# Moving the modulation and query weight loads of a decode attention kernel

## The chip, the cores and the metric

The kernel runs on one core of a Trainium2 chip. The metric is the device time of one execution in microseconds (us); a smaller number is better. The span of an execution is the time from its first to its last instruction in the profile. Heads are counted from 0, so the last one is head 31. Times are medians of several executions. A ratio of two kernels is the mean time of one kernel's runs over that of the other's runs of the same rounds on the same chip, so it is not quite the ratio of the medians that stand beside it.

Engine names in the profile lines: PE is the matrix engine (PEld its weight loads), DVE the vector engine, ACT the scalar engine, POOL the fourth compute engine, SPq the queue of the engine that issues all DMAs here.

## The reference

One token (batch 1, one position, D = 640) goes through one transformer block. Modulation vectors come from a conditioning vector `c`. Attention has 32 heads with their own K and V of 16384 positions and 128 channels, so K and V are 268 MB of the 290 MB that are read.

```python
mod = (silu(c) @ w_mod).reshape(1, 6, 1, 640)          # w_mod: 640 x 3840
sa, ca, ga, sb, cb, gb = (mod[:, i] for i in range(6))
h = layernorm(A_x) * (1 + ca) + sa
q = h @ wq                                             # wq: 640 x 4096, 32 heads of 128
p = softmax(q . k_cache * 128**-0.5)                   # per head, 16384 positions
x = A_x + ga * ((p @ v_cache) @ wo)                    # wo: 4096 x 640
h = layernorm(x) * (1 + cb) + sb
x = x + gb * ((silu(h @ w_gate) * (h @ w_up)) @ w_down)   # 640 x 1728 twice, 1728 x 640
```

Only `sa` and `ca` (the first third of `w_mod`) are needed before attention. `ga`, `sb`, `cb`, `gb` are needed after the last head.

## The kernel before

The program is a list of operations with a position and their dependencies; each engine executes its own in order of position. All DMAs go through one queue, in order, and wait there for the buffers they overwrite. Head `h` has base position `T0 + h * PERIOD`. K and V have two buffers each. DVE multiplies K by the query (in place), folds 128 channels down and reduces; ACT makes the exponent; PE multiplies by V.

```python
# weight region, shared over time
wmod_v = wreg[:, 0:WM_E]...                 # all of w_mod: 2/6 early, 4/6 later
wq_v = [wreg[:, WM_E + i*WQ_E : ...] for i in range(2)]   # ring of two, 4 heads each
wg_v, wu_v, wd_v = ...                      # gate, up, down overlay the same region at the end

d_c  = plan.dma(0.0, c_col[:], c_in[0].rearrange("(c p) -> p c", p=128), "c", noncontig=True)
d_x  = plan.dma(0.1, x_col[:], A_x[0, 0].rearrange("(c p) -> p c", p=128), "x", noncontig=True)
d_wm = plan.dma(0.2, wmod_v[:, :, 0:NA*128], wm_src[:, :, 0:NA*128], "wm")
d_wq[0] = plan.dma(0.3, wq_v[0], wq_src(0), ("wq", 0))
# ...
TB = T0 + 2 * PERIOD - 4.0
d_wm_b = plan.dma(TB, wmod_v[:, :, NA*128:], wm_src[:, :, NA*128:], "wmb")        # about head 4
o_mod_b = op(PE, TBC, lambda e: f_mod(e, NA, NMOD), deps=[d_wm_b, o_sc, o_modc_a])
# ...
for b in range(NQB):                        # 8 blocks of 4 heads: rows of 512 elements, 1024 bytes
    if b > 0:
        d_wq[b] = plan.dma(max(q_pos(b) - 30.0, 1.0), wq_v[b % 2], wq_src(b), ("wq", b % 2), deps=deps)
    o_qmm[b] = op(PE, q_pos(b), f_q, deps=[d_wq[b], o_h])
# ...
for h in range(H):
    d_k[h] = [plan.dma(... base - 25.0, kring[:, s2], kv(A_k, h), ("k", s2), deps=[o_fold1[h - 2]])]
    d_v[h] = [plan.dma(base - 4.9 ..., vring[:, s2, ...], ..., deps=[o_pvlast[h - 2]])]
    d_wo[h] = plan.dma(base + 1.5, woring[:, s2], A_wo[h*128:(h+1)*128, :], ...)
# ... after the last head:
o_abf = op(ACT, TE, ... attn_bf <- attn_ps)            # attention output, then ga, x1, layernorm 2
o_gu = op(PE, TE + 1.2, f_gu, deps=[o_h2, d_wg, d_wu, o_zg, o_zu])
o_dn = op(PE, TE + 1.8, f_down, deps=[o_gum, d_wd, d_wd2])
```

## Time and profile before

| | before |
|---|---|
| time, median of the first 5 runs (range) | 702.09 us (701.16 to 702.38) |
| span in the profiled run | 700.7 us |
| DMA queue's share of 16 engines | 98.1% |
| DVE busy | 618.5 us (88%) |
| first multiply of the last head begins | 652.15 us |
| from there to the end | 48.5 us |

These lines are from the profile page of the kernel before. The digits are the busy share, in tenths, of 40 equal slices of the span; GB/s is what the 16 DMA engines moved in each slice.

```profile
span 700.7 us, 4866 instructions
DMA  7999999999999999999999999999999999999992
GB/s 283 447 428 412 418 430 433 434 420 427 427 437 426 423 428 427 428 424 430 428 427 427 432 427 430 422 434 422 428 430 430 418 430 432 430 430 430 407 402 97
DMA packets 26096, 290.79 MB, mean 415 GB/s; under 512 B 3226, under 2 KB 14170, under 8 KB 16730
q1 hardware_dynamic: 26074, 290.48, 98.1%
...
wreg<-in_A_wq_dram SPq DMA_DIRECT2D x8, 640.0 KB, 29.7
...
wreg<-in_w_mod_dram SPq DMA_DIRECT2D x1, 3200.0 KB, 25.8
```

The reader should see a DMA queue that is full from the second slice to the last but one. While that holds, the time at which a given load lands is set by how much DMA work stands before it in the queue. In the last two lines the columns are the number of loads, KB each, and us from issue to landing.

The trace also records each DMA packet. Grouped by size (mean duration; the sum divided by the 16 engines; left out are the 3456-byte rows of gate and up, 11.2 us, and the 8 KB rows of the K and V loads that come in pieces, 30.2 us):

| packet | what | count before | mean ns | us of 16 engines |
|---|---|---|---|---|
| 2 B | c, x | 1280 | 8 | 0.7 |
| 1024 B | wq | 5120 | 50 | 16.0 |
| 1280 B | wo, w_down | 5824 | 57 | 20.6 |
| 2560 B | w_mod, early part | 640 | 108 | 4.3 |
| 5120 B | w_mod, late part | 640 | 201 | 8.0 |
| 32 KB | K, V | 7808 | 1220 | 595.5 |

The end of the run decides the rest. These are lines of the timeline of the kernel before (start us, duration us, engine, line, operation, output<-input, shapes, count, and in brackets how long the engine had been idle and what ended that):

```profile
652.15 8.69 DVE L410 TENSOR_TENSOR kring<-kring,qbc_sb 128x16384 bf16<-128x16384 bf16 x1 [0.52 <-DMA kring<-in_A_k_cache_dram]
...
673.16 6.72 PE L449 MATMUL psb<-vring,P_sb 128*4 128x512 bf16 x16
680.03 3.92 PE L449 MATMUL psb<-vring,P_sb 128*4 128x512 bf16 x16
...
686.03 0.29 PE L472 MATMUL psb<-On,woring 128*128 128x1 bf16 x5 [0.36 <-ACT On L465]
686.37 0.18 ACT L490 ACTIVATE attn_bf<-psb 128x5 bf16<-128x5 f32 x1 [0.39 <-PE psb L472]
689.56 4.43 PE L513 MATMUL psb<-h_col,wreg 128*128 128x1 bf16 x140 [3.23 <-DVE h_col L500]
695.16 2.83 PE L528 MATMUL psb<-gu_col,wreg 128*128 128x1 bf16 x70 [1.17 <-DVE gu_col L521]
```

The last head's multiply starts 0.5 us after DVE went idle, because its K has just landed. From there a compute chain runs to the end, and gate/up (L513) and down (L528) wait for activations, not for weights. So the time is "when the last K lands" plus a tail of 48.5 us in which the DMA queue still has V and the FFN weights to bring.

### The profile page before, as it was taken

The numbers are of one execution on the slowest core, as the hardware profiler recorded it, in microseconds if no ns is written. First come the engines' busy times: TensorE is split into PE (matmuls) and PEld (weight loads), VectorE is DVE, ScalarE is ACT, GpSimd is POOL, SyncE is SP. The second block draws the span as 40 slices with busy tenths as digits, with TensorE's granted clock in tenths as the row PEclk, the third lists the DMA queues.
The fourth block names the chain that finished last, engine by engine and source line by source line (L and its number), as shares of the span: only waits on it lengthen the run. The fifth ranks groups of instructions, "written<-read, shape, count | busy, mean of one in ns | idle before, by whom it ended". The sixth has DMA issues, their size and how long they took to land.

```text
span 700.7 us, 4866 instructions
## 1 busy us (share of the span) xinstructions
PE 365.1 (52%) x1993; PEld 154.3 (22%) x1993; DVE 618.5 (88%) x220; ACT 84.5 (12%) x321; POOL 251.1 (36%) x76
## 2 busy tenths in 40 slices
PE   0006666644566644446665525665444566555755
PEld 0002223212222211222221212222212222222314
DVE  0799989998999899998999988998999989999931
ACT  1100110111011101111110110111011111101101
POOL 0056633340433354443334404333044433344400
PEclk9999677876776667666666767766676666667975
DMA  7999999999999999999999999999999999999992
GB/s 283 447 428 412 418 430 433 434 420 427 427 437 426 423 428 427 428 424 430 428 427 427 432 427 430 422 434 422 428 430 430 418 430 432 430 430 430 407 402 97
DMA packets 26096, 290.79 MB, mean 415 GB/s; under 512 B 3226, under 2 KB 14170, under 8 KB 16730
## 3 DMA queue, kind: packets, MB, share of 16 engines
q1 hardware_dynamic: 26074, 290.48, 98.1%
q8 instruction: 15, 0.25, 0.1%
q14 instruction: 7, 0.06, 0.0%
HBM read 290.47 MB, written 0.00 MB: 415 GB/s over the span
## 4 chain that ended last, share of the span: by engine, by line
DMA 48%; DVE 39%; PE 6%; issue 3%; POOL 3%; ACT 1%; POOLq 0%; DVEq 0%
DMA kring<-in_A_k_cache_dram 48%; DVE kring L410 22%; DVE f L412 11%; PE psb L449 4%; DVE f L422 3%; POOL Ls L437 2%; DVE S_sb L424 2%; PE psb L513 1%; PE psb L528 0%; ACT acc_sb L455 0%; ACT P_sb L434 0%; POOL gm L430 0%; PE psb L461 0%; ACT R_sb L393 0%; DVE pm L427 0%
## 5 line engine op out<-in xcount | busy, mean ns | idle before, releaser
L449 PE MATMUL psb<-vring,P_sb 128*4 128x512 bf16 x1024 | 298.4, 462 | 29.1 <-DMA vring<-in_A_v_cache_dram 28.2
L410 DVE TENSOR_TENSOR kring<-kring,qbc_sb 128x16384 bf16<-128x16384 bf16 (+1 forms) x35 | 278.6, 7960 | 31.2 <-DMA kring<-in_A_k_cache_dram 27.7
L437 POOL PARTITION_ALL_REDUCE Ls<-rs x32 | 212.3, 6634 | 41.9 <-ACT P_sb L434 41.9
L430 POOL PARTITION_ALL_REDUCE gm<-pm x32 | 36.3, 1136 | 364.1 <-DVE pm L427 353.6
L449 PEld LDWEIGHTS psb<-vring,P_sb 128*4 128x4 bf16 x1024 | 97.6, 98 | 217.3 <-issue 104.6
L412 DVE TENSOR_TENSOR f<-kring 128x8192 bf16<-128x8192 bf16 (+1 forms) x35 | 142.1, 4059 | 1.2
L396 PE MATMUL psb<-R_sb,ones_bf 128*128 128x128 bf16 x32 | 9.2, 286 | 233.9 <-ACT R_sb L393 233.9
L422 DVE TENSOR_TENSOR f<-f 128x4096 bf16<-128x4096 bf16 x64 | 112.5, 1758 | 2.2
L424 DVE TENSOR_REDUCE S_sb<-f 128x128 f32<-128x2048 bf16 x32 | 73.1, 2286 | 1.1
L396 PEld LDWEIGHTS psb<-R_sb,ones_bf 128*128 128x128 bf16 x32 | 3.3, 104 | 236.8 <-ACT R_sb L393 236.8
L455 ACT ACTIVATE acc_sb<-psb 4x512 f32<-4x512 f32 x32 | 18.7, 583 | 244.4 <-PE psb L449 244.4
L461 PE MATMUL psb<-identf,acc_sb 4*128 4x1 f32 x256 | 33.9, 249 | 23.7 <-ACT acc_sb L455 23.7
L461 PEld LDWEIGHTS psb<-identf,acc_sb 4*128 4x128 f32 x256 | 31.2, 188 | 37.0 <-ACT acc_sb L455 37.0
L439 ACT ACTIVATE lnl<-Ls 128x1 f32<-128x1 f32 x32 | 6.5, 202 | 198.2 <-POOL Ls L437 198.2
L472 PE MATMUL psb<-On,woring 128*128 128x1 bf16 x160 | 9.1, 167 | 23.6 <-ACT On L465 23.6
L491 DVE TENSOR_TENSOR tt<-attn_bf,mod_col 128x5 f32<-128x5 bf16 x1 | 0.2, 166 | 15.0 <-ACT attn_bf L490 15.0
L434 ACT ACTIVATE P_sb<-S_sb,nb 128x128 bf16<-128x128 f32 x32 | 12.8, 401 | 1.0
L393 ACT ACTIVATE R_sb<-ident,q_r 128x128 bf16<-128x128 bf16 x32 | 12.4, 386 | 0.0
L472 PEld LDWEIGHTS psb<-On,woring 128*128 128x128 bf16 x160 | 6.4, 101 | 26.3 <-ACT On L465 26.3
L302 DVE TENSOR_SCALAR xc<-x_f,st 128x5 f32<-128x5 f32 x1 | 0.2, 231 | 13.0 <-POOL st L299 13.0
L432 ACT ACTIVATE nb<-gm 128x1 f32<-128x1 f32 x32 | 6.2, 195 | 44.3 <-POOL gm L430 44.3
L399 ACT ACTIVATE qbc_sb<-psb 128x128 bf16<-128x128 f32 x32 | 8.9, 278 | 12.1 <-PE psb L396 12.1
(59 smaller groups left out, 76.5 us busy)
## 6 DMA issues: line engine op xcount, KB each, us to landing
kring<-in_A_k_cache_dram SPq DMA_DIRECT2D x31, 4096.0 KB, 26.7
vring<-in_A_v_cache_dram SPq DMA_DIRECT2D x30, 4096.0 KB, 30.7
vring<-in_A_v_cache_dram SPq DMA_DIRECT2D x8, 1024.0 KB, 21.5
wreg<-in_A_wq_dram SPq DMA_DIRECT2D x8, 640.0 KB, 29.7
woring<-in_A_wo_dram SPq DMA_DIRECT2D x32, 160.0 KB, 28.6
kring<-in_A_k_cache_dram SPq DMA_DIRECT2D x4, 1024.0 KB, 13.4
wreg<-in_w_mod_dram SPq DMA_DIRECT2D x1, 3200.0 KB, 25.8
wreg<-in_B_w_gate_dram SPq DMA_DIRECT2D x1, 2160.0 KB, 24.7
```

What stands on the lines that cost most here:

```text
L396: o_qbcmm[h] = op(PE, base - 14.8 if h > 0 else 2.7, lambda e, s2=s2: e.matmul(qbc_ps[s2], lhsT=ones_bf[:], rhs=R_sb[:, s2], start=True, s ...
L410: o_m = op(DVE, base + 3.3 * c, lambda e, ksl=ksl, qb=qb: e.tensor_tensor(out=ksl, in0=ksl, in1=qb, op=ALU.mult), deps=[d_k[h][c], o_qbc[h ...
L412: o_f = op(DVE, base + 3.3 * c + 2.2 + (6.6 if npc == 1 else 0.0), lambda e, ksl=ksl, c=c, KP=KP: e.tensor_tensor(out=f1[:, c * KP:(c + 1) ...
L422: prev = op(DVE, base + 13.3 + i, lambda e, w=w: e.tensor_tensor(out=f1[:, :, 0:w], in0=f1[:, :, 0:w], in1=f1[:, :, w:2 * w], op=ALU.add), ...
L424: o_red[h] = op(DVE, base + 17.0, lambda e, w=w, s2=s2: e.tensor_reduce(out=S_sb[:, s2], in_=f1[:, :, 0:w], axis=AX.X, op=ALU.add), deps=[ ...
L430: o_gm[h] = op(POOL, base + 19.6, lambda e, h=h: e.partition_all_reduce(gm[:, h:h + 1], pm[:, h:h + 1], channels=128, reduce_op=bass.bass_ ...
L434: o_exp[h] = op(ACT, base + 20.4, lambda e, h=h, s2=s2: e.activation(out=P_sb[:, s2], in_=S_sb[:, s2], func=ACTF.Exp, scale=SCALE, bias=nb ...
L437: o_L[h] = op(POOL, base + 21.0, lambda e, h=h: e.partition_all_reduce(Ls[:, h:h + 1], rs[:, h:h + 1], channels=128, reduce_op=bass.bass_i ...
L449: last = e.matmul(acc_ps[s2], lhsT=P_sb[:, s2, 4 * j:4 * j + 4], rhs=vring[:, s2, 4 * j:4 * j + 4, :].rearrange("p a d -> p (a d)"), start ...
L455: o_acc[h] = op(ACT, base + 39.5, lambda e, s2=s2: e.activation(out=acc_sb[:, s2, :], in_=acc_ps[s2], func=ACTF.Copy), deps=[o_pvlast[h], ...
L461: last = e.matmul(OT_ps[:, h:h + 1], lhsT=acc_sb[:, s2, 128 * i:128 * (i + 1)], rhs=identf[:, i:i + 1], start=(i == 0), stop=(i == 3))
L472: last = e.matmul(attn_ps[:, cc:cc + 1], lhsT=woring[:, s2, 128 * cc:128 * (cc + 1)], rhs=On[:, h:h + 1], start=(h == 0 and cc == 0), stop ...
```

## The change

The intent: make `wq` two loads instead of eight (4 heads, then the other 28 with 7168-byte rows); start with `w_mod` instead of the tiny `c` and `x`; load the late four sixths of `w_mod` after the last K into the K buffer that is then free; split the down projection so that it can start on most of its weights. The core of the diff, with cuts:

```diff
-        wmod_v = wreg[:, 0:WM_E]...
-        wq_v = [wreg[:, WM_E + i * WQ_E: ...]... for i in range(2)]
+        wma_v = wreg[:, 0:WMA_E]...
+        wq0_v = wreg[:, WMA_E:WMA_E + WQ0_E]...
+        wqr_v = wreg[:, 0:WQR_E]... if H > HB else None
+            wmb_v = kring[:, (H - 2) % 2]...[:, 0:WMB_E]...
...
-        d_c = plan.dma(0.0, c_col[:], ...)
-        d_x = plan.dma(0.1, x_col[:], ...)
-        d_wm = plan.dma(0.2, wmod_v[:, :, 0:NA * 128], ...)
-        d_wq[0] = plan.dma(0.3, wq_v[0], wq_src(0), ("wq", 0), ...)
+        d_wm = plan.dma(0.0, wma_v, wm_src[:, :, 0:2 * D], "wm", ...)
+        d_c = plan.dma(0.1, c_col[:], ...)
+        d_x = plan.dma(0.15, x_col[:], ...)
+        d_wq0 = plan.dma(0.3, wq0_v, wq_src[:, :, 0:HB * 128], "wq0", ...)
...
-        TB = T0 + 2 * PERIOD - 4.0
+            TB = TLAST + 2.0              # TLAST: base of the last head
+            TBC = TLAST + 41.5
...
+            d_wqr = plan.dma(2.3, wqr_v, wq_src[:, :, HB * 128:H * 128], "wqr", deps=[o_mod, o_qmm0], ...)
+            o_qmm1, o_qbf1, o_qr1 = q_ops(TQR, wqr_v, HB, H, d_wqr, "1")
...
+        d_wm_b = plan.dma(TB, wmb_v, wm_src[:, :, 2 * D:6 * D], "wmb", deps=[o_fold1[H - 2]], ...)
+        o_mod_b = op(PE, TBC, lambda e: f_mod(e, wmb_v, NA, NMOD, NA), deps=[d_wm_b] + mb_deps, ...)
...
-        o_dn = op(PE, TE + 1.8, f_down, deps=[o_gum, d_wd, d_wd2], name="down")
+        o_dn_a = op(PE, TE + 1.8, lambda e: f_down(e, 0, nA), deps=[o_gum, d_wd], name="down_a")
+        o_dn = op(PE, TE + 1.85, lambda e: f_down(e, nA, FCH), deps=[o_dn_a, d_wd_b, d_wd2], name="down")
```

More of the change, by code (lines that the diff above doesn't have):

```diff
@@ L180, in build @@
         x_col = sb("x_col", [128, KC], BF16)
-        WM_E = KC * 6 * D
-        WQ_E = KC * HB * 128
-        WREG_E = max(WM_E + 2 * WQ_E, 2 * KC * F + FCH * D)
+        LATE_MB = (TT * 128 >= KC * 4 * D) and H >= 3
+        NA = 2 * KC
+        WMA_E = KC * 2 * D
+        WQ0_E = KC * HB * 128
+        WQR_E = KC * (H - HB) * 128
+        WMB_E = KC * 4 * D
+        FFN_E = 2 * KC * F + FCH * D
+        WREG_E = max(WMA_E + WQ0_E, WQR_E, FFN_E) + (0 if LATE_MB else WMB_E)
         wreg = sb("wreg", [128, WREG_E], BF16)
-        wmod_v = wreg[:, 0:WM_E].rearrange("p (k n) -> p k n", k=KC)
-        wq_v = [wreg[:, WM_E + i * WQ_E: WM_E + (i + 1) * WQ_E].rearrange("p (k n) -> p k n", k=KC) for i in range(2)]
+        wma_v = wreg[:, 0:WMA_E].rearrange("p (k n) -> p k n", k=KC)
+        wq0_v = wreg[:, WMA_E:WMA_E + WQ0_E].rearrange("p (k n) -> p k n", k=KC)
+        wqr_v = wreg[:, 0:WQR_E].rearrange("p (k n) -> p k n", k=KC) if H > HB else None
         wg_v = wreg[:, 0:KC * F].rearrange("p (k n) -> p k n", k=KC)
@@ L190, in build @@
         kring = sb("kring", [128, 2, TT, 128], BF16)
+        if LATE_MB:
+            wmb_v = kring[:, (H - 2) % 2].rearrange("p t d -> p (t d)")[:, 0:WMB_E].rearrange("p (k n) -> p k n", k=KC)
+        else:
+            wmb_v = wreg[:, WREG_E - WMB_E:WREG_E].rearrange("p (k n) -> p k n", k=KC)
         vring = sb("vring", [128, 2, TT, 128], BF16)
@@ L260, in build @@
             fill=0.0, base=0, channel_multiplier=-1), deps=[o_onesf], name="identf")
-        d_c = plan.dma(0.0, c_col[:], c_in[0].rearrange("(c p) -> p c", p=128), "c", noncontig=True, name="dma_c")
-        d_x = plan.dma(0.1, x_col[:], A_x[0, 0].rearrange("(c p) -> p c", p=128), "x", noncontig=True, name="dma_x")
-        NA = 2 * KC
         wm_src = w_mod.rearrange("(k p) n -> p k n", p=128)
-        d_wm = plan.dma(0.2, wmod_v[:, :, 0:NA * 128], wm_src[:, :, 0:NA * 128], "wm", name="dma_wmod_a")
-        def wq_src(b):
-            return A_wq[:, b * HB * 128:(b + 1) * HB * 128].rearrange("(k p) n -> p k n", p=128)
-        d_wq = [None] * NQB
-        d_wq[0] = plan.dma(0.3, wq_v[0], wq_src(0), ("wq", 0), name="dma_wq0")
+        d_wm = plan.dma(0.0, wma_v, wm_src[:, :, 0:2 * D], "wm", name="dma_wmod_a")
+        d_c = plan.dma(0.1, c_col[:], c_in[0].rearrange("(c p) -> p c", p=128), "c", noncontig=True, name="dma_c")
+        d_x = plan.dma(0.15, x_col[:], A_x[0, 0].rearrange("(c p) -> p c", p=128), "x", noncontig=True, name="dma_x")
+        wq_src = A_wq.rearrange("(k p) n -> p k n", p=128)
+        d_wq0 = plan.dma(0.3, wq0_v, wq_src[:, :, 0:HB * 128], "wq0", name="dma_wq0")
         o_tbl = op(ACT, 0.0, lambda e: e.preload_act_table_set("natural_log_exp_and_others"), name="tbl")
@@ L278, in build, with f_mod @@
         o_sc = op(DVE, 0.5, lambda e: e.tensor_tensor(out=silu_c[:], in0=c_col[:], in1=rr[:], op=ALU.mult), deps=[o_rr], name="silu_c")
-        def f_mod(e, j0, j1):
+        def f_mod(e, wv, j0, j1, jofs):
             last = None
@@ L283, in f_mod @@
                 for k in range(KC):
-                    last = e.matmul(mod_ps[:, j:j + 1], lhsT=wmod_v[:, k, 128 * j:128 * (j + 1)], rhs=silu_c[:, k:k + 1],
+                    last = e.matmul(mod_ps[:, j:j + 1], lhsT=wv[:, k, 128 * (j - jofs):128 * (j - jofs + 1)], rhs=silu_c[:, k:k + 1],
                                     start=(k == 0), stop=(k == KC - 1))
             return last
-        o_mod = op(PE, 1.0, lambda e: f_mod(e, 0, NA), deps=[d_wm, o_sc], name="mod_mm_a")
+        o_mod = op(PE, 1.0, lambda e: f_mod(e, wma_v, 0, NA, 0), deps=[d_wm, o_sc], name="mod_mm_a")
         o_modc_a = op(ACT, 1.5, lambda e: e.activation(out=mod_col[:, 0:NA], in_=mod_ps[:, 0:NA], func=ACTF.Copy), deps=[o_mod], name="mod_col_a")
-        TB = T0 + 2 * PERIOD - 4.0
-        d_wm_b = plan.dma(TB, wmod_v[:, :, NA * 128:], wm_src[:, :, NA * 128:], "wmb", name="dma_wmod_b")
-        TBC = min(TB + 2.5 * PERIOD, T0 + H * PERIOD - 8.0)
-        o_mod_b = op(PE, TBC, lambda e: f_mod(e, NA, NMOD), deps=[d_wm_b, o_sc, o_modc_a], name="mod_mm_b")
-        o_modc = op(ACT, TBC + 0.2, lambda e: e.activation(out=mod_col[:, NA:], in_=mod_ps[:, NA:NMOD], func=ACTF.Copy), deps=[o_mod_b], name="mod_col_b")
+        TLAST = T0 + (H - 1) * PERIOD
+        if LATE_MB:
+            TB = TLAST + 2.0
+            TBC = TLAST + 41.5
+        else:
+            TB = T0 + 2 * PERIOD - 4.0
+            TBC = min(TB + 2.5 * PERIOD, T0 + H * PERIOD - 8.0)
+        mb_deps = [o_sc, o_modc_a]
+        d_wm_b = None
         o_onep = op(DVE, 1.6, lambda e: e.tensor_scalar_add(out=onep[:, 0, :], in0=mod_col[:, KC:2 * KC], scalar1=1.0), deps=[o_modc_a], name="onep_a")
-        o_onep_b = op(DVE, TBC + 5.0, lambda e: e.tensor_scalar_add(out=onep[:, 1, :], in0=mod_col[:, 4 * KC:5 * KC], scalar1=1.0), deps=[o_modc], name="onep_b")
+        o_onep_b_pos = TBC + 0.4
         def layernorm_ops(pos, src_f32, src_dep, rs_col, tag, xc_t, want_rs=None):
@@ L323, in build @@
         o_h = op(DVE, 1.8, lambda e: e.tensor_tensor(out=h_col[:], in0=tt1[:], in1=mod_col[:, 0:KC], op=ALU.add), deps=[o_t1, o_modc_a], name="h_col")
-        o_qmm = [None] * NQB
-        o_qbf = [None] * NQB
-        o_qr = [None] * NQB
-        def q_pos(b):
-            return 2.0 if b == 0 else T0 + b * HB * PERIOD - 22.0
-        for b in range(NQB):
-            if b > 0:
-                deps = [o_qmm[b - 2]] if b >= 2 else []
-                d_wq[b] = plan.dma(max(q_pos(b) - 30.0, 1.0), wq_v[b % 2], wq_src(b), ("wq", b % 2), deps=deps, name="dma_wq%d" % b)
-            def f_q(e, b=b):
-                last = None
-                for hl in range(HB):
-                    hh = b * HB + hl
-                    for k in range(KC):
-                        last = e.matmul(q_ps[:, hh:hh + 1], lhsT=wq_v[b % 2][:, k, 128 * hl:128 * (hl + 1)], rhs=h_col[:, k:k + 1],
-                                        start=(k == 0), stop=(k == KC - 1))
-                return last
-            o_qmm[b] = op(PE, q_pos(b), f_q, deps=[d_wq[b], o_h], name="q_mm%d" % b)
-            o_qbf[b] = op(ACT, q_pos(b) + 0.1, lambda e, b=b: e.activation(
-                out=q_bf[:, b * HB:(b + 1) * HB], in_=q_ps[:, b * HB:(b + 1) * HB], func=ACTF.Copy), deps=[o_qmm[b]], name="q_bf%d" % b)
-            o_qr[b] = op(ACT, q_pos(b) + 0.2, lambda e, b=b: e.activation(
-                out=q_r32[:, b * HB:(b + 1) * HB], in_=q_bf[:, b * HB:(b + 1) * HB], func=ACTF.Copy), deps=[o_qbf[b]], name="q_r32_%d" % b)
@@ new lines, in f_q, with q_ops @@
+        def f_q(e, wv, h0, h1):
+            last = None
+            for hh in range(h0, h1):
+                for k in range(KC):
+                    last = e.matmul(q_ps[:, hh:hh + 1], lhsT=wv[:, k, 128 * (hh - h0):128 * (hh - h0 + 1)], rhs=h_col[:, k:k + 1],
+                                    start=(k == 0), stop=(k == KC - 1))
+            return last
+        def q_ops(pos, wv, h0, h1, ddep, tag):
+            o_mm = op(PE, pos, lambda e: f_q(e, wv, h0, h1), deps=[ddep, o_h], name="q_mm" + tag)
+            o_bf = op(ACT, pos + 0.1, lambda e: e.activation(out=q_bf[:, h0:h1], in_=q_ps[:, h0:h1], func=ACTF.Copy), deps=[o_mm], name="q_bf" + tag)
+            o_r = op(ACT, pos + 0.2, lambda e: e.activation(out=q_r32[:, h0:h1], in_=q_bf[:, h0:h1], func=ACTF.Copy), deps=[o_bf], name="q_r32_" + tag)
+            return o_mm, o_bf, o_r
@@ new lines, in build @@
+        o_qmm0, o_qbf0, o_qr0 = q_ops(2.0, wq0_v, 0, HB, d_wq0, "0")
+        o_qmm_last, o_qbf_last = o_qmm0, o_qbf0
+        o_qr = [o_qr0] * H
+        if H > HB:
+            TQR = T0 + 0.6 * PERIOD
+            d_wqr = plan.dma(2.3, wqr_v, wq_src[:, :, HB * 128:H * 128], "wqr", deps=[o_mod, o_qmm0], name="dma_wq_rest")
+            o_qmm1, o_qbf1, o_qr1 = q_ops(TQR, wqr_v, HB, H, d_wqr, "1")
+            for hh in range(HB, H):
+                o_qr[hh] = o_qr1
+            o_qmm_last, o_qbf_last = o_qmm1, o_qbf1
+            assert T0 + HB * PERIOD - 15.0 > TQR + 0.3
@@ L394, in build @@
                 out=R_sb[:, s2], in_=ident[:], func=ACTF.Copy, scale=q_r32[:, h:h + 1]),
-                deps=[o_qr[b], o_ident, o_qbcmm[h - 2] if h >= 2 else None], name="R%d" % h)
+                deps=[o_qr[h], o_ident, o_qbcmm[h - 2] if h >= 2 else None], name="R%d" % h)
             o_qbcmm[h] = op(PE, base - 14.8 if h > 0 else 2.7, lambda e, s2=s2: e.matmul(
@@ L477, in build @@
         TE = T0 + (H - 1) * PERIOD + 42.0
-        TW = max(T0 + (H - 1) * PERIOD + 2.0, q_pos(NQB - 1) + 0.5, TBC + 0.5)
-        wdeps = [o_qmm[NQB - 1], o_mod_b]
+        d_wm_b = plan.dma(TB, wmb_v, wm_src[:, :, 2 * D:6 * D], "wmb",
+                          deps=[o_fold1[H - 2]] if LATE_MB else [], name="dma_wmod_b")
+        o_mod_b = op(PE, TBC, lambda e: f_mod(e, wmb_v, NA, NMOD, NA), deps=[d_wm_b] + mb_deps, name="mod_mm_b")
+        o_modc = op(ACT, TBC + 0.2, lambda e: e.activation(out=mod_col[:, NA:], in_=mod_ps[:, NA:NMOD], func=ACTF.Copy), deps=[o_mod_b], name="mod_col_b")
+        o_onep_b = op(DVE, o_onep_b_pos, lambda e: e.tensor_scalar_add(out=onep[:, 1, :], in0=mod_col[:, 4 * KC:5 * KC], scalar1=1.0), deps=[o_modc], name="onep_b")
+        TW = TLAST + 2.5 if LATE_MB else max(TLAST + 2.5, TBC + 0.5)
+        wdeps = [o_qmm_last, o_mod] + ([] if LATE_MB else [o_mod_b])
         d_wg = plan.dma(TW, wg_v, B_wg.rearrange("(k p) n -> p k n", p=128), "wg", deps=wdeps, name="dma_wg")
@@ L482, in build @@
         nfull = FCH - 1 if FLAST < 128 else FCH
-        d_wd = plan.dma(TW + 0.02, wd_v[:, 0:nfull, :], B_wd[0:nfull * 128, :].rearrange("(k p) n -> p k n", p=128), "wd",
-                        deps=wdeps, name="dma_wd")
+        nA = max(1, nfull - 1)
+        wd_src = lambda k0, k1: B_wd[k0 * 128:k1 * 128, :].rearrange("(k p) n -> p k n", p=128)
+        d_wd = plan.dma(TW + 0.02, wd_v[:, 0:nA, :], wd_src(0, nA), "wd", deps=wdeps, name="dma_wd")
+        d_wd_b = plan.dma(TW + 0.03, wd_v[:, nA:nfull, :], wd_src(nA, nfull), "wdb", deps=wdeps, name="dma_wd_b") if nfull > nA else None
         d_wd2 = None
         if nfull < FCH:
-            d_wd2 = plan.dma(TW + 0.03, wd_v[0:FLAST, nfull, :], B_wd[nfull * 128:F, :], "wd2",
+            d_wd2 = plan.dma(TW + 0.04, wd_v[0:FLAST, nfull, :], B_wd[nfull * 128:F, :], "wd2",
                              deps=wdeps, name="dma_wd2")
@@ L501, in build @@
                   deps=[o_t2], name="h2_col")
-        o_zg = op(DVE, TE - 1.0, lambda e: e.memset(g_ps[:, 0:FCH], 0.0), deps=[o_modc], name="zero_g")
-        o_zu = op(DVE, TE - 0.9, lambda e: e.memset(u_ps[:, 0:FCH], 0.0), deps=[o_qbf[NQB - 1]], name="zero_u")
-        assert TE - 1.0 > q_pos(NQB - 1) + 0.3 and TE - 1.0 > TBC + 5.3
+        o_zg = op(DVE, TE + 0.05, lambda e: e.memset(g_ps[:, 0:FCH], 0.0), deps=[o_modc], name="zero_g")
+        o_zu = op(DVE, TE - 0.9, lambda e: e.memset(u_ps[:, 0:FCH], 0.0), deps=[o_qbf_last], name="zero_u")
         def f_gu(e):
@@ L521, in build, with f_down @@
         o_gum = op(DVE, TE + 1.7, lambda e: e.tensor_tensor(out=gu_col[:], in0=u_ps[:, 0:FCH], in1=sg[:], op=ALU.mult), deps=[o_sg], name="gu")
-        def f_down(e):
+        def f_down(e, k0, k1):
             last = None
             for cc in range(KC):
-                for k in range(FCH):
+                for k in range(k0, k1):
                     kw = 128 if k < FCH - 1 else FLAST
                     last = e.matmul(f_ps[:, cc:cc + 1], lhsT=wd_v[0:kw, k, 128 * cc:128 * (cc + 1)], rhs=gu_col[0:kw, k:k + 1],
-                                    start=(k == 0), stop=(k == FCH - 1))
+                                    start=(k == 0 and cc == 0), stop=(k == FCH - 1 and cc == KC - 1), skip_group_check=True)
             return last
-        o_dn = op(PE, TE + 1.8, f_down, deps=[o_gum, d_wd, d_wd2], name="down")
+        o_dn_a = op(PE, TE + 1.8, lambda e: f_down(e, 0, nA), deps=[o_gum, d_wd], name="down_a")
+        o_dn = op(PE, TE + 1.85, lambda e: f_down(e, nA, FCH), deps=[o_dn_a, d_wd_b, d_wd2], name="down")
         o_t3 = op(DVE, TE + 1.9, lambda e: e.tensor_tensor(out=tt3[:], in0=f_ps[:, 0:KC], in1=mod_col[:, 5 * KC:6 * KC], op=ALU.mult),
@@ L546, in build @@
             dump("h_col", h_col[:], [o_h])
-            dump("q_r32", q_r32[:], [o_qr[NQB - 1]])
+            dump("q_r32", q_r32[:], [o_qr[H - 1]])
             dump("pm", pm[:], [o_max[H - 1]])
```

## The prediction

> **What bounds it now.** The DMA engines. The page gives their queue 98.1% of 16 engines' span, at about 428 GB/s. The packet records of the trace, summed and divided by 16 engines, give 689 us of work in a 700.7 us span. DVE is second: 19.3 us a head (timeline, early heads), against 19.97 us of DMA a head (K and V, 256 packets of 32 KB at 1220 ns, 128 of 1280 B at 57 ns). The time-ordered chain shows the end: K of the last head lands about 651.65, and from there a fixed compute chain of 49 us runs: multiply and folds (652.15 to 671.5), exponent, PV to 684, output projection to 686.3, second layernorm, gate/up from 689.56 (140 matmuls, 4.44 us), down from 695.16 (2.85 us), output. The last weight packet moves at 690.1, 5 us before it is needed. So the time is "when K31 lands" plus a compute tail, and DMA work queued behind K31 is nearly free.
>
> **What the change does to DMA ahead of K31.**
> 1. w_mod's late part (640 packets of 5120 B, 201 ns: 8.0 us of all engines) moves from about 83 us to behind V31. K31 gains 8.0 us.
> 2. wq: seven of eight 640 KB loads, 4480 packets of 1024 B at 50 ns (14.0 us), become 640 packets of 7168 B. From 8192 B at 315 ns I estimate 276 ns, 11.05 us. Gain 2.95 us. The Trainium skill ("DMA: Bandwidth & Descriptors", section "Why small descriptors are slow (HBM only)") states a fixed overhead per packet; the trace agrees: 1 KB takes 50 ns where a 1 KB share of a 32 KB packet takes 38.
> 3. Start: bulk packets begin at 5.5 us now, behind 1280 two-byte packets of c and x. With w_mod first they begin about 2.7 us; the small packets still cost something inside the stream. Estimated net gain 1.2 us (0.2 to 2.1). The late c and x cost nothing: layernorm 1 waits for POOL until 17.1 us.
>
> K31 should land near 639.5. DVE alone would be ready near 621, so DMA stays the limit. The large wq load (11 us) fits between K1 and V0: K2 should then land near 60 us, when DVE wants it (61.6).
>
> **What it costs in the tail.** The late modulation matmuls (100, at 31.7 ns from the gate/up group: 3.2 us) now stand on PE between the last output projection and gate/up, and ACT's copy of their result stands before attn_bf. About 3.4 us are added to the chain. The w_mod load itself lands near 667 to 670, needed about 674. Up lands near 680, needed 680.8; down near 686, needed 686.4: close, perhaps a stall of 1 us. Splitting down helps only if that stall appears.
>
> **Sum.** -8.0 -2.95 -1.2 +3.4 = -8.7 us: 702.1 becomes 693.4 us (-1.2%). Range 689.5 to 697.5. Chances: faster by over 2% 0.06, within 2% 0.92, slower 0.02.
>
> **What would show each step.** 4480 fewer packets of 1024 B; packets of 7168 B near 276 ns; first multiply of head 31 about 640.0; bulk packets from 2.7 us; modulation matmuls between the last output projection and attn_bf; gate/up starting 41 us after head 31's multiply begins, not 37.4; last weight packet near 686.
>
> **What would make it wrong.** Gate/up or down waiting several us for weights, as the DMA end nearly meets the compute end; SP blocked on the big wq load (it waits for the first q matmul, about 20.6 us) so that the DMA queue runs dry; two-byte packets costing more in the stream; slower 7 KB packets; DVE getting extra waits and becoming the limit.

## The result, and the profile after

The changed kernel took 694.45 us (median of 7 runs, 694.27 to 695.59) where the kernel before, over 13 runs in all, took 701.3 us (700.85 to 702.38). The ratio is 0.9904, with a 95% interval from 0.9894 to 0.9914: a gain of about 1%, small but clear of the noise. A second set of runs gave 694.54 us and 0.9899.

The same lines of the page, of the changed kernel:

```profile
span 692.7 us, 4851 instructions
DMA  8999999999999999999999999999999999999995
GB/s 296 427 440 423 431 433 430 424 432 427 424 439 429 430 428 430 433 426 431 433 426 431 430 430 428 423 441 426 429 428 431 430 429 431 427 433 416 419 407 210
DMA packets 22176, 290.79 MB, mean 420 GB/s; under 512 B 3146, under 2 KB 9610, under 8 KB 12810
q1 hardware_dynamic: 22154, 290.48, 98.8%
...
wreg<-in_A_wq_dram SPq DMA_DIRECT2D x1, 4480.0 KB, 21.0
...
kring<-in_w_mod_dram SPq DMA_DIRECT2D x1, 3200.0 KB, 27.1
```

The bytes are the same and the packets are 3920 fewer. The queue is as full as before, now into the last slice, where 210 GB/s stand in place of 97. The packet records show 640 packets of 7168 B with a mean of 276.3 ns (11.05 us of 16 engines) and 640 of 1024 B (1.9 us). The last weight packet ends at 686.7 us, 6.0 us before the end of the span; before it was 689.3, 11.3 us before the end. (The packet times in the prediction, 5.5, 2.7 and 690.1 us, are counted from about 0.8 us before the span's start; by the span's start they are 4.7, 1.9 and 689.3.)

The end in the timeline of the changed kernel:

```profile
641.62 8.69 DVE L419 TENSOR_TENSOR kring<-kring,qbc_sb 128x16384 bf16<-128x16384 bf16 x1 [0.51 <-DMA kring<-in_A_k_cache_dram]
...
662.63 7.53 PE L458 MATMUL psb<-vring,P_sb 128*4 128x512 bf16 x24
670.31 1.89 PE L458 MATMUL psb<-vring,P_sb 128*4 128x512 bf16 x8
...
674.28 0.28 PE L481 MATMUL psb<-On,woring 128*128 128x1 bf16 x5 [0.36 <-ACT On L474]
674.42 2.70 PE L289 MATMUL psb<-silu_c,kring 128*128 128x1 bf16 x100
677.24 0.17 ACT L507 ACTIVATE attn_bf<-psb 128x5 bf16<-128x5 f32 x1
680.28 0.17 DVE L517 TENSOR_TENSOR h_col<-tt,mod_col 128x5 bf16<-128x5 f32 x1
681.42 4.41 PE L529 MATMUL psb<-h_col,wreg 128*128 128x1 bf16 x140 [4.31 <-DMA wreg<-in_B_w_up_dram]
687.00 3.06 PE L544 MATMUL psb<-gu_col,wreg 128*128 128x1 bf16 x70 [1.18 <-DVE gu_col L537]
```

Three things are to be seen. The last head's multiply starts at 641.62 instead of 652.15, 10.5 us earlier. The 100 modulation matmuls (L289) stand between the output projection (L481) and the copy of its result (attn_bf), which now comes 2.96 us after the projection's start instead of 0.34. And gate/up (L529) now begins when the up weights land: its input `h_col` was ready at 680.45, the first matmul starts at 681.42. In the packet records the last packet of gate and up ends 39.1 us after the last multiply begins; before the change it was 31.2 us. The tail from the last multiply to the end is 51.1 us instead of 48.5.

### The profile page after: what moved, and what is told of

It is laid out like the page before. It is cut to its first block, busy times and chain, and to the rows that moved or that the text cites. A ratio compares the mean times of both kernels' runs of the same rounds, so it can differ in the third digit from the quotient of the medians.

```text
span 692.7 us, 4851 instructions
## 1 busy us (share of the span) xinstructions
PE 358.7 (52%) x1993; PEld 152.3 (22%) x1993; DVE 618.7 (89%) x220; ACT 82.9 (12%) x309; POOL 256.1 (37%) x76
## 4 chain that ended last, share of the span: by engine, by line
DMA 62%; DVE 32%; issue 3%; SPq 1%; PE 1%; ACT 0%; POOL 0%; POOLq 0%; DVEq 0%
DMA kring<-in_A_k_cache_dram 58%; DVE kring L419 20%; DVE f L421 10%; DMA wreg<-in_B_w_up_dram 4%; SPq L71 1%; PE psb L529 1%; DVE f L431 1%; PE psb L544 0%; DVE S_sb L433 0%; PE psb L338 0%; ACT P_sb L443 0%; POOL st L308 0%; ACT R_sb L402 0%; POOL st L316 0%; POOL gm L439 0%
## 5 line engine op out<-in xcount | busy, mean ns | idle before, releaser
L458 PE MATMUL psb<-vring,P_sb 128*4 128x512 bf16 x1024 | 292.9, 455 | 10.5 <-DMA vring<-in_A_v_cache_dram 9.6
L446 POOL PARTITION_ALL_REDUCE Ls<-rs x32 | 234.0, 7314 | 35.2 <-ACT P_sb L443 35.2
L439 POOL PARTITION_ALL_REDUCE gm<-pm x32 | 19.6, 613 | 354.7 <-DVE pm L436 344.2
L338 PE MATMUL psb<-h_col,wreg 128*128 128x1 bf16 x160 | 4.6, 165 | 28.7 <-DMA wreg<-in_A_wq_dram 18.9
L481 PE MATMUL psb<-On,woring 128*128 128x1 bf16 x160 | 8.9, 166 | 19.9 <-ACT On L474 19.9
L481 PEld LDWEIGHTS psb<-On,woring 128*128 128x128 bf16 x160 | 6.2, 97 | 22.6 <-ACT On L474 22.6
L338 PEld LDWEIGHTS psb<-h_col,wreg 128*128 128x128 bf16 x160 | 4.4, 104 | 28.9 <-DMA wreg<-in_A_wq_dram 19.1
## 6 DMA issues: line engine op xcount, KB each, us to landing
woring<-in_A_wo_dram SPq DMA_DIRECT2D x32, 160.0 KB, 28.5
kring<-in_A_k_cache_dram SPq DMA_DIRECT2D x4, 1024.0 KB, 10.3
```

Of the source, the lines that this page charges most:

```text
L439: o_gm[h] = op(POOL, base + 19.6, lambda e, h=h: e.partition_all_reduce(gm[:, h:h + 1], pm[:, h:h + 1], channels=128, reduce_op=bass.bass_ ...
L446: o_L[h] = op(POOL, base + 21.0, lambda e, h=h: e.partition_all_reduce(Ls[:, h:h + 1], rs[:, h:h + 1], channels=128, reduce_op=bass.bass_i ...
L458: last = e.matmul(acc_ps[s2], lhsT=P_sb[:, s2, 4 * j:4 * j + 4], rhs=vring[:, s2, 4 * j:4 * j + 4, :].rearrange("p a d -> p (a d)"), start ...
L481: last = e.matmul(attn_ps[:, cc:cc + 1], lhsT=woring[:, s2, 128 * cc:128 * (cc + 1)], rhs=On[:, h:h + 1], start=(h == 0 and cc == 0), stop ...
```

## The experiments

Eleven kernels ran, each timed in five rounds beside the kernel before. Unless said otherwise each is the changed kernel with one edit. All gave correct results. They ran in four sets on four chips: the control with e1 to e3; e4, e5, e6 and e8; e7 and e9; e10. So most are compared with a control of another chip; the medians of the kernel before in the four sets are 701.60, 701.45, 701.41 and 701.33.

| run | edit to the changed kernel | median us (range) | ratio to before | last multiply starts |
|---|---|---|---|---|
| a0_after | none | 694.54 (694.40 to 694.68) | 0.9899 | 641.66 |
| e1_wq_1k | wq rest in 1024 B rows | 696.96 (696.63 to 697.13) | 0.9932 | 643.95 |
| e2_wq_512b | wq rest in 512 B rows | 699.32 (699.25 to 699.46) | 0.9967 | 646.55 |
| e3_mod_mid | late w_mod back in mid-run | 698.75 (698.38 to 699.88) | 0.9964 | 649.39 |
| e4_cx_first | c and x first again | 694.89 (694.63 to 694.97) | 0.9903 | 641.96 |
| e5_mod_split | modulation matmuls split | 694.44 (694.27 to 694.57) | 0.9897 | 641.60 |
| e6_down_whole | down not split | 695.11 (694.27 to 696.31) | 0.9908 | 641.48 |
| e8_cx_rows | c and x as rows | 692.93 (692.63 to 693.19) | 0.9877 | 639.43 |
| e7_tail | gate, up, down follow their weights | 693.10 (692.83 to 693.18) | 0.9880 | 641.47 |
| e9_best | e7_tail and e8_cx_rows together | 691.49 (691.13 to 691.88) | 0.9857 | 639.23 |
| e10_order | e9_best, loops of down turned round | 690.56 (690.23 to 690.87) | 0.9844 | 639.34 |

The interval of each ratio is about 0.0014 to either side, that is 1 us; for differences below 1 us the text leans on the profiled times of single events, and on the span that the record lists for each timed execution, and says so.

### The control

> The changed kernel again, unedited, as the control for the kernels beside it on the same chip. Expected 694.4 us, a ratio of 0.990 to the kernel before, first multiply of head 31 between 641 and 642 us.

It came as expected: 694.54 us. Three lines of its timeline, to which the runs below are compared:

```profile
641.66 8.69 DVE L419 TENSOR_TENSOR kring<-kring,qbc_sb 128x16384 bf16<-128x16384 bf16 x1 [0.52 <-ACT acc_sb L464]
...
680.67 0.17 DVE L517 TENSOR_TENSOR h_col<-tt,mod_col 128x5 bf16<-128x5 f32 x1
681.38 4.41 PE L529 MATMUL psb<-h_col,wreg 128*128 128x1 bf16 x140 [3.87 <-DMA wreg<-in_B_w_up_dram]
```

(The multiply doesn't depend on the `acc_sb` that is named as its releaser; that only ended in the same moment. In the other runs the same wait of 0.5 us is put down to the load of K.) The last multiply began between 641.47 and 641.66 us in the five profiles whose loads before it are the same (after, a0, e5, e6, e7); that is the scatter of this event.

### Does the packet size of wq matter, and how much?

```diff
-            d_wqr = plan.dma(2.3, wqr_v, wq_src[:, :, HB * 128:H * 128], "wqr", deps=[o_mod, o_qmm0], ...)
+            WC = 512          # e2_wq_512b: 256
+            d_wqr = [plan.dma(2.3 + 0.01 * i, wqr_v[:, :, i*WC:(i+1)*WC], wq_src[:, :, HB*128 + i*WC:HB*128 + (i+1)*WC],
+                              ("wqr", i), deps=[o_mod, o_qmm0], ...) for i in range((H - HB) * 128 // WC)]
```

> The late 28 heads of wq arrive in seven loads with 1024-byte rows instead of one load with 7168-byte rows; place in the queue, bytes and the one q matmul block are unchanged. Theory (each packet costs the DMA engines a fixed time, and DMA work ahead of the last K is paid in full): 4480 packets at 50 ns instead of 640 at 276 ns, 14.0 instead of 11.05 us of the 16 engines, so the first multiply of head 31 comes 3.0 us later and the time is 2.5 to 3.5 us longer. Rival (the gain of the wq edit lies in fewer q matmul blocks and waits on PE and ACT, not in packets): time unchanged within 0.5 us.

> As the 1024-byte version but fourteen loads with 512-byte rows, 8960 packets. Theory: from 50 ns at 1024 B and 276 ns at 7168 B a line gives about 31 ns a packet at 512 B, 17.4 us of the engines, so head 31's first multiply comes 6.3 us later than in the changed kernel and the time is 5.5 to 7 us longer. If the packet cost is not linear the step will be larger. Rival (packets do not matter): unchanged.

The first multiply of the last head in the timelines of e1_wq_1k and of e2_wq_512b:

```profile
643.95 8.69 DVE L421 TENSOR_TENSOR kring<-kring,qbc_sb 128x16384 bf16<-128x16384 bf16 x1 [0.51 <-DMA kring<-in_A_k_cache_dram]
```

```profile
646.55 8.69 DVE L421 TENSOR_TENSOR kring<-kring,qbc_sb 128x16384 bf16<-128x16384 bf16 x1 [0.52 <-DMA kring<-in_A_k_cache_dram]
```

Against the control's 641.66 the last K is used 2.29 us and 4.89 us later, 600 us after the loads in question, and the times are 2.4 and 4.8 us longer. In e1 nearly every multiply from head 3 on is 2.3 us later than in the control, in e2 4.9. A delay put into a full queue at 40 us is still there at 640. The rival, that fewer matmul blocks and waits made the gain, falls: those were unchanged here, apart from the number of loads that the one block waits for.

The size was smaller than expected. The two runs agree on one number: 3840 more packets cost 2.29 us and 8320 more cost 4.89, so one packet more costs 16 * 2.29 / 3840 = 9.5 ns and 16 * 4.89 / 8320 = 9.4 ns of one engine. The edits also add 6 and 13 loads, in the same proportion, so a cost per load (0.38 us) would fit the times as well. The starts of the packets in the traces decide it: an engine starts a packet every 272.8 ns on average at 7168 bytes (control), every 47.1 ns at 1024 (e1) and every 28.2 ns at 512 (e2), over the middle four fifths of these packets, and the distance is the same inside a load as across the border of two (47.0 and 47.1 in e1, 28.3 and 28.2 in e2). So the cost is the packet's: the three sizes lie on one line to 1 ns, with 9.4 ns at size zero. The recorded durations give a larger cost: 1024-byte packets sum to 16.1 us with a mean of 50.4 ns in e1, 512-byte packets to 19.0 us with a mean of 33.8 ns in e2, so that all durations together grow by 3.3 and 8.25 us. Since they are longer than the distance of two starts (50.4 against 47.1 ns, 33.8 against 28.2), small packets of one engine overlap in the records, and their durations may not simply be added. Put together from the times at the last K, with the larger packets at their recorded 11.05 us, one 1024-byte packet cost 47.6 ns ((11.05 + 2.29) * 16 / 4480) and one 512-byte packet 28.5, close to the distances. The kernel before shows the same cost: at six of its wq loads the next multiply comes 1.9 us later than the regular 19.9 (21.77 us, for instance), and 1.88 us for 640 packets is 47 ns each.

### What is the late place of w_mod worth, and what does it cost?

```diff
-        LATE_MB = (TT * 128 >= KC * 4 * D) and H >= 3
+        LATE_MB = False                                  # load and matmuls at about head 4, as in the kernel before
-            wmb_v = wreg[:, WREG_E - WMB_E:WREG_E]...
+            wmb_v = wreg[:, 0:WMB_E]...                  # free after the q matmuls
-                          deps=[o_fold1[H - 2]] if LATE_MB else [], ...)
+                          deps=[o_qmm_last, o_mod], ...)
```

> The changed kernel with the late part of w_mod put back to the middle of the run (loaded after head 3's K into the weight region, its matmuls there too), all else kept. Theory: 8.0 us of DMA are again ahead of the last K, so head 31's first multiply comes 8.0 us later (about 649.6), but the tail after it loses the modulation matmuls (2.7 us) and the wait for the up weights (0.9 us), so the tail from that multiply is 47 to 48 us instead of 51.1, and the time is 4 to 5 us longer than the changed kernel's. Rival (the move costs nothing in the tail, since the tail ends when the DMA does): the time is 8 us longer. Rival 2 (moving it is worthless, total DMA work being the same): time unchanged.

Three lines of its timeline:

```profile
649.39 8.69 DVE L419 TENSOR_TENSOR kring<-kring,qbc_sb 128x16384 bf16<-128x16384 bf16 x1 [0.49 <-DMA kring<-in_A_k_cache_dram]
...
685.34 4.44 PE L529 MATMUL psb<-h_col,wreg 128*128 128x1 bf16 x140 [3.24 <-DVE h_col L517]
690.95 3.06 PE L544 MATMUL psb<-gu_col,wreg 128*128 128x1 bf16 x70 [1.17 <-DVE gu_col L537]
```

The last multiply is 7.73 us later than in the control, gate/up waits for its input and not for weights, and the tail is 47.3 us (span 696.7) against the control's 51.0. So the late load gives 7.7 us and takes 3.7 back, or 3.5 by the times, whose medians differ by 4.2 us, inside the 4 to 5 expected; the profile is of the fastest of the five executions. Both rivals, 8 us and nothing, fall.

### What is the new order at the start worth?

```diff
-        d_wm = plan.dma(0.0, ...)    d_c = plan.dma(0.1, ...)    d_x = plan.dma(0.15, ...)
+        d_wm = plan.dma(0.2, ...)    d_c = plan.dma(0.0, ...)    d_x = plan.dma(0.1, ...)
```

> The changed kernel with the two small loads c and x put back ahead of the first w_mod load. The prediction gave the new order 1.2 us; the book-keeping after the first four runs leaves only about 0.5 us for it (first multiply of head 31 came 10.5 us earlier in all, the w_mod move accounts for 7.7 and the packets for 2.3). Expected now: 0.2 to 0.8 us slower than the changed kernel, that is a ratio to the kernel before near 0.9907. Rival (the prediction): 1.2 us slower.

The last multiply in its timeline:

```profile
641.96 8.69 DVE L419 TENSOR_TENSOR kring<-kring,qbc_sb 128x16384 bf16<-128x16384 bf16 x1 [0.50 <-DMA kring<-in_A_k_cache_dram]
```

The last multiply began 0.30 us later than in the control and the median was 0.35 us longer. That is below what the interval resolves, so the sign is not proved by the times; but every multiply from head 3 on is 0.3 to 0.4 us later than in the control, and 641.96 lies outside the scatter of 641.47 to 641.66. A value of 1.2 us is unlikely and 0.3 fits. Why so little? The busy share of two stretches says it. First the kernel before, then the changed kernel (stretch in us, its length, then each engine's busy us and instructions, granted PE clock, DMA share, GB/s):

```profile
0.00:5.00 5.00, 0.00 (x0) 0.00 (x0) 0.53 (x3) 1.49 (x2) 0.40 (x5) 1.00 0.15 4
5.00:10.00 5.00, 0.00 (x0) 0.00 (x0) 0.00 (x0) 0.30 (x2) 0.00 (x0) 1.00 0.97 366
```

```profile
0.00:5.00 5.00, 0.00 (x0) 0.00 (x0) 0.00 (x0) 1.28 (x1) 0.39 (x5) 1.00 0.58 182
5.00:10.00 5.00, 0.78 (x30) 0.81 (x30) 0.53 (x3) 0.51 (x3) 0.00 (x0) 1.00 0.74 220
```

Bulk data does start earlier (182 GB/s instead of 4 in the first 5 us), but the 1280 two-byte packets then stand in the middle of the stream and the next 5 us drop from 366 to 220 GB/s. The dead time was moved, not removed.

### Removing the two-byte packets

```diff
-        d_c = plan.dma(0.1, c_col[:], c_in[0].rearrange("(c p) -> p c", p=128), "c", noncontig=True, ...)
+        d_cr = plan.dma(0.1, c_row[:], c_in[0].rearrange("(c p) -> c p", p=128), "c", ...)    # 5 rows of 256 bytes
+        o_ct = op(PE, 0.16, lambda e: e.matmul(psb[6][:, 0:KC], lhsT=c_row[:], rhs=ident[0:KC, 0:KC], ...), deps=[d_cr, o_ident])
+        d_c = op(ACT, 0.18, lambda e: e.activation(out=c_col[:], in_=psb[6][:, 0:KC], func=ACTF.Copy), deps=[o_ct])
         # and the same for x, through psb[7]
```

> The changed kernel with c and x each loaded as five rows of 256 bytes and turned into columns by two small matmuls, in place of 1280 packets of 2 bytes. Theory (the slices show about 1.0 MB fewer bytes moved between 5 and 10 us, 2.3 us of the engines, while the two-byte packets run): head 31's first multiply and the time come 1.7 to 2.5 us earlier. Rival (the packets cost what their recorded durations sum to, 0.7 us of 16 engines): 0.7 us earlier.

The stretches of e8_cx_rows, in the same columns as those before, and its last multiply:

```profile
0.00:5.00 5.00, 0.00 (x0) 0.00 (x0) 0.00 (x0) 1.28 (x1) 0.39 (x5) 1.00 0.60 178
5.00:10.00 5.00, 0.00 (x0) 0.00 (x0) 0.00 (x0) 0.00 (x0) 0.00 (x0) 1.00 1.04 363
...
639.43 8.69 DVE L425 TENSOR_TENSOR kring<-kring,qbc_sb 128x16384 bf16<-128x16384 bf16 x1 [0.53 <-DMA kring<-in_A_k_cache_dram]
```

The hole is gone. The last multiply begins at 639.43, 2.2 us earlier than in the control, and the time is 1.6 us shorter, just under the range expected; the tail grew a little, as the up weights came only 1.8 us earlier (gate/up at 679.61 instead of 681.38). The two-byte packets cost about 2.2 * 16 / 1280 = 28 ns each (an estimate that puts the whole difference down to them), not the 8 to 9 ns of their records. Part of the 2.2 us may not be theirs: from head 9 to head 17 the lead over the control is 1.8 to 1.9 us (1.7 to 1.8 in e9_best, which has this edit too), and it grows at head 21, whose late K (see the open point below) is 0.6 us late here and 1.3 in the control. With 1.85 us the estimate is 23 ns, so 23 to 28 ns it is. The rival of 0.7 us falls.

### Is the modulation block a cost of its own in the tail?

```diff
-        o_mod_b = op(PE, TBC, lambda e: f_mod(e, wmb_v, NA, NMOD, NA), ...)                     # 100 matmuls
-        o_modc = op(ACT, TBC + 0.2, ...)
+        o_mod_g = op(PE, TBC, f_modg, ...)                              # 25 matmuls for ga, in another PSUM bank
+        o_modc_g = op(ACT, TBC + 0.2, ...)                              # attn_bf follows here
+        o_mod_b = op(PE, TBC + 0.1, lambda e: f_mod(e, wmb_v, NG, NMOD, NA), deps=[o_mod_g])    # 75 matmuls
+        o_modc = op(ACT, TE + 0.6, ...)                                 # between layernorm's square and log
```

(PSUM is the memory that PE writes its results to. The first 25 go to another bank of it, so that ACT doesn't copy from the bank that PE is writing.)

> The changed kernel with the late modulation matmuls split: 25 for the gate of attention before attn_bf, the other 75 behind it, under the second layernorm, with their copy between layernorm's square and log. The compute chain to gate/up gets about 2 us shorter. Theory A (gate/up in the changed kernel starts when the up weights land, so the modulation block is hidden almost wholly behind that landing): gate/up still starts near 681.3 and the time moves by less than 0.5 us. Theory B (the block is a cost of its own in the tail, as the prediction added it): about 2 us faster.

```profile
674.82 0.76 PE L494 MATMUL psb<-silu_c,kring 128*128 128x1 bf16 x25
675.64 2.05 PE L289 MATMUL psb<-silu_c,kring 128*128 128x1 bf16 x75
...
678.66 0.17 DVE L527 TENSOR_TENSOR h_col<-tt,mod_col 128x5 bf16<-128x5 f32 x1
681.33 4.41 PE L539 MATMUL psb<-h_col,wreg 128*128 128x1 bf16 x140 [3.63 <-DMA wreg<-in_B_w_up_dram]
```

In these lines of its timeline, the 75 matmuls run under the second layernorm and `h_col` begins at 678.66, 2.0 us earlier than in the control (680.67). Gate/up still begins at 681.33. The time is the same, 694.44 against 694.54. So in the changed kernel the tail is paced by the landing of the up weights, and the modulation block is nearly hidden behind that landing. Theory A holds. The two paths lie close together, though: in e1_wq_1k and e4_cx_first, whose last V matmuls ran at a lower granted clock (0.73 against the control's 0.78), gate/up started 0.06 us after `h_col` and did not wait for the up weights.

### Does the split of the down projection help?

```diff
-        nA = max(1, nfull - 1)
+        nA = nfull
-        o_dn_a = ...; o_dn = ...
+        o_dn = op(PE, TE + 1.8, lambda e: f_down(e, 0, FCH), deps=[o_gum, d_wd, d_wd_b, d_wd2], name="down")
```

> The changed kernel without the split of the down projection: one matmul block that waits for all of its weights. Theory (the last weights land about 688.8 us, after the activations are ready at 687.0): down begins about 688.8 and needs its whole 2.9 us there, so 1.2 to 1.8 us slower than the changed kernel. Rival (the split gains nothing since the weights have landed): unchanged.

The expectation missed. The down line of its timeline:

```profile
687.23 2.81 PE L544 MATMUL psb<-gu_col,wreg 128*128 128x1 bf16 x70 [1.48 <-DMA wreg<-in_B_w_down_dram]
```

All of w_down had landed by 687.2, 0.3 us after the activations, and the one block took 2.81 us where the two of the split took 3.06. Both end near 690.05. The profiled span is 692.7 in both. The timed runs scatter from 694.27 to 696.31, but the record gives the span of each: 692.5 to 693.0, against 692.6 to 692.9 in the control. The excess of the two long ones (695.64 with a span of 692.7, 696.31 with 693.0) lies outside the program's span. So the split brought nothing, as the rival said. I had read the last block of the changed kernel (10 matmuls in 1.25 us, in its chain of work) as a wait for weights; the last experiment shows what it mostly is.

### A tail that follows its weights

```diff
+        o_gate = op(PE, TE + 1.2, lambda e: f_gu(e, wg_v, g_ps), deps=[o_h2, d_wg, o_zg], name="gate")
+        o_gu = op(PE, TE + 1.25, lambda e: f_gu(e, wu_v, u_ps), deps=[o_gate, d_wu, o_zu], name="up")
         # exp, reciprocal and product for silu now depend on o_gate alone
+        WDP = [(0, 4), (4, 8), (8, 11), (11, nfull)]          # four loads of w_down, four down blocks
         # together with the modulation split of e5_mod_split
```

> The changed kernel with its tail made to follow the arrival of the weights: modulation matmuls split as in the earlier run, gate and up as two matmul blocks that each wait for their own weights, and down in four blocks that each wait for their own part of w_down. Theory (after the last K the changed kernel's tail is paced by the landing of the up weights at 681.3 and of the last w_down at about 687.2, and everything behind those landings is compute that can be drawn ahead): activations for down ready about 684, down ends about 0.6 us after the last landing instead of 2.9, time 1.5 to 2.5 us shorter than the changed kernel. Rival (the tail is a fixed compute chain): unchanged, as splitting the modulation block alone was.

```profile
678.32 2.25 PE L538 MATMUL psb<-h_col,wreg 128*128 128x1 bf16 x70 [1.14 <-DVE h_col L527]
681.27 2.22 PE L538 MATMUL psb<-h_col,wreg 128*128 128x1 bf16 x70 [0.70 <-DMA wreg<-in_B_w_up_dram]
...
685.98 0.56 PE L554 MATMUL psb<-gu_col,wreg 128*128 128x1 bf16 x15 [0.61 <-DMA wreg<-in_B_w_down_dram]
687.10 1.34 PE L554 MATMUL psb<-gu_col,wreg 128*128 128x1 bf16 x15 [0.55 <-DMA wreg<-in_B_w_down_dram]
```

In its timeline, gate is done before the up weights land, and each later block waits for its own weights only. The time is 1.4 us shorter than the control's, a little less than the 1.5 to 2.5 expected; the last block of 15 matmuls took 1.34 us where the one before, also of 15, took 0.56.

> That tail together with c and x loaded as rows. Theory: the two gains lie in different places (DMA work at the start, compute behind the last landing at the end) and add up: 3 to 4.5 us shorter than the changed kernel, 690 to 691.5 us, a ratio to the kernel before of 0.984 to 0.986. If they share one limit, no better than the better of the two alone.

The two gains add: 1.4 and 1.6 us alone, 3.05 us together (691.49 us), at the lower edge of what was expected for the gain. They lie at the two ends of the run.

### Why the last block of down is slow

The last 64 rows of w_down (1728 = 13 * 128 + 64) make five of its matmuls 64 rows high. In the loops of every version so far each of them follows matmuls of 128 rows, and all but the last stand before such matmuls again.

```diff
-            for cc in range(KC):
-                for k in range(k0, k1):
+            for k in range(k0, k1):
+                for cc in range(KC):
```

> The best version so far with one more edit: the loops of the down projection are turned round, so that the five matmuls with 64 rows stand together at the end instead of each between matmuls of 128 rows. In the version before, the last block of 15 took 1.34 us where 15 matmuls of 128 rows took 0.56. Theory (each change between 64 and 128 rows costs PE over 0.1 us): the last block takes 0.6 to 0.8 us and the time is 0.5 to 0.8 us shorter, about 690.9 us. Rival (the last block waits for weights while it runs): 1.3 us again and no gain.

The last block of down in e9_best, then in e10_order (timelines):

```profile
685.43 1.34 PE L560 MATMUL psb<-gu_col,wreg 128*128 128x1 bf16 x15 [0.55 <-DMA wreg<-in_B_w_down_dram]
```

```profile
685.88 0.63 PE L560 MATMUL psb<-gu_col,wreg 128*128 128x1 bf16 x15 [0.82 <-DMA wreg<-in_B_w_down_dram]
```

The block takes 0.63 us and the time falls to 690.56 us, 0.9 us less than e9_best, somewhat more than the block alone explains and than the 0.5 to 0.8 expected. The two ran on different chips and their ratios overlap; the spans do not (688.5 to 689.2 against 689.4 to 690.1). The order of the loops by itself did nothing: the three blocks before, all of 128 rows, take 0.69, 0.69 and 0.56 us in e9_best and 0.70, 0.69 and 0.56 in e10_order. With the old order the height changes nine times in the block, with the new one once; 0.71 us over eight changes is 0.09 us each. The Trainium skill ("TensorEngine Tiling (Array Packing)", section "Key Properties") says that changing the tiling mode drains the engine. The numbers fit that, but no run here shows the drain itself, or that a matmul of 64 rows runs in another mode.

This last version is the fastest: a ratio of 0.9844 (0.9831 to 0.9858) to the kernel before, where the change as given had 0.9904.

## Why the prediction was right

The prediction said 693.4 us, within 689.5 to 697.5; the result was 694.45. Its mechanism held: time is the landing of the last K plus a tail, every us of DMA work ahead of the last K is paid, and work queued behind it is paid only in part. That the number came within 1.1 us is in part luck: it started from 702.1 us, the median of the first five runs of the kernel before, where 13 runs give 701.3, and this made up for 0.8 of the 1.85 us by which the gain was set too high. Term by term:

| term | predicted | measured | by |
|---|---|---|---|
| late w_mod behind the last K | -8.0 | -7.7 | e3_mod_mid against a0_after |
| wq in larger packets | -2.95 | -2.3 | e1_wq_1k against a0_after |
| order at the start | -1.2 | -0.3 | e4_cx_first against a0_after |
| first multiply of head 31, sum of these | -12.15 | -10.3 (seen: -10.5) | both profiles |
| tail | +3.4, perhaps 1 more | +3.7 (3.5 by the times) | e3_mod_mid against a0_after |
| sum | -8.7 | -6.6 (seen: -6.85, median against median) | |

- The late load was sized well: 8.0 us of packets, 7.7 us at the last K.
- The step "Gain 2.95 us" for wq was too large. The packet estimate itself was right to the nanosecond (276.3 measured for 276), but the 50 ns of the small packets it was set against include overlap: in use they cost 47 to 48. The Trainium skill's fixed cost per packet ("DMA: Bandwidth & Descriptors", "Why small descriptors are slow (HBM only)") is borne out, at 9.4 to 9.5 ns a packet in both runs.
- The step "Estimated net gain 1.2 us" for the start was the least sound. The prediction gives no working for it. Its 5.5 and 2.7 us make 2.8 us at the start, so it left about 1.6 us for the two-byte packets inside the stream; e8_cx_rows puts them at 1.85 to 2.2 us, nearly as much as at the start. Its own list of risks named this one, and the 0.3 us measured lies in its range of 0.2 to 2.1.
- The tail's +3.4 was close, but described as a compute cost, and there the agreement is partly luck. The 100 matmuls took 2.65 us in the control instead of 3.2. From e3_mod_mid to the control the chain from the last multiply to `h_col` grew by 3.3 us, 0.6 of it in V matmuls at another clock; another 0.5 us is the wait for the up weights. The prediction's own sign, gate/up 41 us after the last multiply begins, came out as 39.8. The better account is e5_mod_split's: a shorter modulation block brings nothing, because gate/up then waits the longer for the up weights. The prediction had this meeting point in its numbers ("Up lands near 680, needed 680.8") and called it a possible stall of 1 us; the profile after shows 0.97.
- The tail grew by only 2.6 us from profile to profile (48.5 to 51.1), less than the 3.7 above. The profile before is of the slowest of its executions (702.38 us). In the profile before, the last head's V matmuls took 10.8 us (673.16 to 683.95), in the profile after 9.6. The granted PE clock over these stretches was 0.72 before and 0.83 after; in other versions the same matmuls took 10.7 us at 0.73 (e4_cx_first) and 9.4 at 0.84 (e6_down_whole); length times clock is 7.8 to 7.9 us in all four. So their length follows the clock granted in that stretch, and it varies between versions whose matmuls there are the same. Why the clock differs, no run settles.
- The prediction's 640.0 for the first multiply was 641.62, as follows mostly from the two oversized gains. Its 686 for the last weight packet, 685.2 when counted from the span's start, was 686.7.

One point stays open. In nearly all versions one late K, most often that of head 21, lands 0.6 to 1.5 us behind the regular 19.9 us a head and the delay stays for good. In the profile after, a 16 KB instruction packet lies on a DMA engine at that time (435.9 us), and single K packets near such instruction packets took 1.7 us instead of 1.2. That they are the cause is only argued. Since kernels before and after both show it (21.2 and 21.4 us between two multiplies), it hardly bears on their difference, but it does blur differences below 1 us, as in e8_cx_rows.

## What to carry to other kernels

When the DMA queue never runs dry, add up the DMA work ahead of the last load that the critical chain waits for: moving a load behind it brings that point forward by nearly the load's whole transfer time (7.7 of 8.0 us here) and lengthens the tail by a part of it (3.5 to 3.7 us here). Once the last weights are the thing that is waited for, a shorter compute block in the tail brings nothing unless each matmul block waits for its own weights alone. Cost small packets by a run that changes their number, or by the distance of their starts, not by the sum of their recorded durations, which was too high for 512-byte packets and far too low for two-byte ones. Moving a hole in the stream to another place is not removing it.

## What the Trainium skill lacked or had wrong

- "DMA: Bandwidth & Descriptors", "Specifications", gives 512 B as the least transfer for line rate. Here a 512-byte packet cost 28.5 ns of one engine, 16 * 512 / 28.5 = 287 GB/s for all, where the K and V stream ran at about 430 GB/s. Going from 1024-byte to 7168-byte rows still gained 2.3 us.
- The same page, "Why small descriptors are slow (HBM only)", gives the fixed cost per packet as about 3 bus cycles, not in time. The runs show 9.4 to 9.5 ns per packet between 512 and 7168 B.
- The same page, "Rules for kernel authors", says that a non-contiguous last dimension becomes one descriptor per element, which the 1280 two-byte packets confirm, but not what one costs: 23 to 28 ns of an engine here in a full stream, by an estimate, and not much more at the start (e4_cx_first is only 0.3 us behind the control).
- No page was found to say that the recorded durations of small packets on one engine overlap and may not be summed: 8320 more packets raised their sum by 8.25 us and the landing of the last K by 4.89.
- "TensorEngine Tiling (Array Packing)", "Key Properties", names the drain at a change of mode without a figure. Alternating 64-row and 128-row matmuls cost about 0.09 us a change here (1.34 us against 0.63 for the same 15 matmuls).
